# A decode block on one core: w_down in three transfers, a semaphore for each store, q in three chunks, nine matmuls fewer

## The chip, the cores and the metric

The kernel runs on one core of a Trainium2 chip. Its five engines are called by the profile's names: PE (TensorE, matmuls; PEld is its weight loads), DVE (VectorE), ACT (ScalarE), POOL (GpSimd) and SP (SyncE, which here only issues transfers). Sixteen DMA engines carry the transfers. The metric is the device time of one execution in microseconds (us); smaller is better.

## The reference

Two tokens (batch 2, one position each, width 640) pass through one block with modulation from a condition vector `c`. What is computed, shortened:

```python
mod = (silu(c) @ w_mod).reshape(2, 6, 1, -1)
sa, ca, ga, sb, cb, gb = (mod[:, i] for i in range(6))
h = layernorm(x) * (1 + ca) + sa
q = (h @ wq)                              # 32 heads of 192
p = softmax(q k^T * 192 ** -0.5)          # over the last 1024 cached keys
x = x + ga * ((p v) @ wo)
h = layernorm(x) * (1 + cb) + sb
x = x + gb * ((gelu(h @ w_gate) * (h @ w_up)) @ w_down)
```

All inputs are bfloat16. wq is 640 x 6144, wo 6144 x 640, w_gate and w_up 640 x 1536, w_down 1536 x 640, w_mod 640 x 3840. K and V have 32 heads per batch row, and 1024 rows of 192 of each head are used. That is 77 MB of reads for two tokens.

## The kernel before, in words

The scheduler in the kernel (`_Sched`) is a recorder: each operation is put into the list of its engine in the order in which the program calls it, with the operations that it depends on. At the end the lists are written out (`S.emit`), and each engine runs its list strictly in order, with a wait on a semaphore ahead of an operation where one is needed. All compute engines count on one semaphore each; each transfer, or group of transfers, has its own. One recorded operation can hold many matmuls, and those who wait for it wait for its last.

All large transfers are issued by SP from one list (every issue has line 378): w_mod, c, wq, four of K, four of V (6144 KB each), wo in two parts with eight small ones (`wx`) between, w_gate, w_up, w_down. A ring of slots in `store` is used again and again, so a later transfer waits until PE has read the slot's earlier contents.

The stages in order of time:

- Modulation and first LayerNorm (L510, L478 to L497), while w_mod and wq come in.
- **q** (L533): `hT` is the normalised input, transposed, in five parts of 128. PE's array is used as four column groups of 32, so group j makes the j-th quarter (1536 columns) of q. Each quarter is made in four chunks of `QC` = 384 columns, one in each of the PSUM banks 4 to 7: 5 x 4 x 4 = 80 matmuls. ACT and DVE copy the four chunks to `qC` in turn (L541, L543), a selection by 16 matmuls (L552) spreads q over the partitions, and ACT writes it to `qbc`. The third K transfer is issued after the q matmuls, since it overwrites wq.
- A loop of 57 matmuls that nobody reads (L691, L693) keeps PE busy until K arrives.
- **Scores**: for each half tile DVE multiplies K by `qbc` (L571), PE sums groups of columns with an identity matrix (L590), DVE finishes the sum (L604). Between them PE runs groups of four matmuls without a reader (L583).
- **Softmax and PV** (L610 to L637, L649), then the normalisation of the attention output (L662, L666) and its selection into rows: `p_sel(0)` and `p_sel(1)` (L674), eight matmuls each. Between the two stand `warm(3, 1)`, after the second `warm(6, 1)`: three and six matmuls of 384 columns into bank 1, which nobody reads (L563). The chunks are copied (L541, L543), transposed by DVE (L738, L744), and multiplied by wo (L782, in two groups with the sixteen `wx` matmuls of L790 between).
- **Second LayerNorm** (L799 to L497), then gate and up projections (L822), GELU (L829), the product (L836) and its transposes (L840).
- **Down projection** (L852): w_down has twelve rows of 1280 B on each partition, `WD_SPLIT = [6, 3, 2, 1]` says how many rows a transfer brings. Each transfer has its own semaphore, and the matmuls of a group of rows wait for it: eight matmuls for a row. `WD_WARM` gives the number of matmuls without a reader behind each group, all zero.
- **End**: DVE multiplies and adds (L861, L863), SP and ACT each store one half of the output (L378), both on the semaphore `sem_out`, and SP waits until it has 32 (L870).

Of the kernel before, what the change touches and what calls it, by code (L numbers as in the profile page):

```python
# [193 lines left out]
def bass_adaLN_cond__sliding_block_cached__geglu_ffn__decode_kernel(  # L194
# [21 lines left out]
    SQ = 32  # L216
# [17 lines left out]
    RN = HM * Dh  # L234
    QC = 2 * Dh
    NQC = RN // QC
    SCALE = float(Dh) ** -0.5
    EPS = 1e-5
    GC = 512 // JH
# [12 lines left out]
    assert sum(WO_SPLIT) == NB and sum(OT_SPLIT) == NB  # L252
    WU_SPLIT = [5]
    assert sum(WU_SPLIT) == KT
    WD_SPLIT = [6, 3, 2, 1]
    AT_SPLIT = [6, 6]
    assert sum(AT_SPLIT) == FT
    assert sum(WD_SPLIT) == FT
    NG = 2
# [5 lines left out]

    WO_WARM = [4, 9]
    WU_WARM = [5]
    WD_WARM = [0, 0, 0, 0]
    K_WARM = 14

    es = ExitStack()
    with es:
        S = _Sched(nc, es)
# [5 lines left out]
        wq_v = r1.rearrange("p (k n) -> p k n", k=KT)  # L279
# [12 lines left out]
        Qsel = aux_f(0, 2 * HM * P).rearrange("p (b m n) -> p b m n", b=2, m=HM)  # L292
        qC = aux_f(2 * HM * P, RN)
# [28 lines left out]
        sc = sb("sc", [P, DN], BF16)  # L322
# [9 lines left out]
        hT = sb("hT", [P, KT, SQ], BF16)  # L332
# [17 lines left out]
        ps = es.enter_context(nc.psum_tensor("ps", [P, 8, 512], F32))  # L350

        BK_T = 2
        BK_O = 3
        BK_C = 4
        BK_W = 4
        BK_H = 4
# [5 lines left out]
        def bank(k):  # L362
            return ("bank", k)
# [8 lines left out]
        sem_wu = [S.sem("d_wu%d" % i) for i in range(len(WU_SPLIT))]  # L372
        sem_wd = [S.sem("d_wd%d" % i) for i in range(len(WD_SPLIT))]
        sem_ring = [S.sem("d_ring%d" % i) for i in range(4)]
        sem_out = S.sem("d_out")

        def k_dma(dst, src):
            return lambda e: e.dma_start(dst, src)  # L378
# [5 lines left out]
        def dram_rows(v):  # L384
# [10 lines left out]
             reads=[("S", 0, 0, 0), ("S", 0, 0, 1), ("S", 0, 1, 0), ("S", 0, 1, 1)], writes=["ident_f"], name="ident_f")  # L395
        S.op("pool", lambda e: e.tensor_copy(out=ident_b[:, :], in_=ident_f[:, :]),
             reads=["ident_f"], writes=["ident_b"], name="ident_b")
# [4 lines left out]
             reads=["ident_f"], writes=["G32"], name="G32")  # L402
        S.op("dve", lambda e: e.tensor_reduce(out=M32[:, :], in_=ident_f[:, :].rearrange("p (h t) -> p h t", t=QP), axis=AX.X, op=ALU.add),
             reads=["ident_f"], writes=["M32"], name="M32")
# [3 lines left out]
             reads=["G32"], writes=["Bsel"], name="Bsel")  # L408
# [3 lines left out]
             reads=["M32"], writes=["DS"], name="DS")  # L412
# [4 lines left out]
             reads=["ident_f"], writes=["Osel"], name="Osel")  # L417
        for b in range(2):
            S.op("dve", (lambda b: lambda e: e.tensor_copy(
                out=SEL[:, b, :, BS * b:P:SQ], in_=G32[:, :].rearrange("p (j m) -> p m j", m=HM)))(b),  # L420
                reads=["G32"], writes=["SEL"], name="SEL%d" % b)
        for b in range(2):
            for m in range(HM):
# [3 lines left out]
                    reads=["ident_f"], writes=["Qsel"], name="Qsel%d%d" % (b, m))  # L427
# [7 lines left out]
        keep = {}  # L435
# [91 lines left out]
        for i, (ka, kb) in enumerate(wq_of):  # L527
            def f(e, ka=ka, kb=kb):
                last = None
                for k in range(ka, kb):  # L530
                    for c in range(NQC):
                        for j in range(NJ):
                            last = e.matmul(ps[SQ * j:SQ * j + SQ, BK_H + c, 0:QC], lhsT=hT[:, k, :],  # L533
                                            rhs=wq_v[:, k, RN * j + QC * c:RN * j + QC * (c + 1)],
                                            start=(k == 0), stop=(k == KT - 1), tile_position=(0, SQ * j), skip_group_check=True)
                return last
            keep["q"] = S.op("pe", f, reads=["hT", ("wq", i)], writes=[bank(BK_H + c) for c in range(NQC)], name="q%d" % i)

        def move(eng, dst, src, reads, writes, name):
            if eng == "act":  # L540
                S.op("act", lambda e: e.activation(out=dst, in_=src, func=ACTF.Copy), reads=reads, writes=writes, name=name)  # L541
            else:
                S.op("dve", lambda e: e.tensor_copy(out=dst, in_=src), reads=reads, writes=writes, name=name)  # L543

        for c in range(NQC):
            move(("act", "dve")[c % 2], qC[:, QC * c:QC * (c + 1)], ps[:, BK_H + c, 0:QC], [bank(BK_H + c)], [("qC", c)], "qC%d" % c)

        def f(e):
            last = None
# [2 lines left out]
                    last = e.matmul(ps[:, BK_O, b * Dh:(b + 1) * Dh], lhsT=Qsel[:, b, m, :], rhs=qC[:, m * Dh:(m + 1) * Dh],  # L552
                                    start=(m == 0), stop=(m == HM - 1), skip_group_check=True)
            return last
        S.op("pe", f, reads=[("qC", c) for c in range(NQC)] + ["Qsel"], writes=[bank(BK_O)], name="qsel")
        move("act", qbc[:, :, :].rearrange("p b d -> p (b d)"), ps[:, BK_O, 0:2 * Dh], [bank(BK_O)], ["qbc"], "qbc")
        load_kv(3, deps=keep["wq_dma"] + [keep["q"]])

        def warm(n, bk):
            def f(e):  # L560
                last = None
                for _ in range(n):
                    last = e.matmul(ps[:, bk, 0:2 * Dh], lhsT=ident_b[:, :], rhs=qbc[:, :, :].rearrange("p b d -> p (b d)"),  # L563
                                    start=True, stop=True)
                return last
            if n:
                S.op("pe", f, reads=["ident_b", "qbc"], writes=[bank(bk)], name="warm")
# [40 lines left out]
        def softmax(b):  # L608
# [8 lines left out]
            S.op("dve", lambda e: e.tensor_scalar(out=gx[:, :, :], in0=gm[:, :].unsqueeze(2).broadcast_to([1, H, QP]),  # L617
                                                  scalar1=-SCALE, scalar2=None, op0=ALU.mult),
                 reads=["gm"], writes=["gx"], name="gx%d" % b)
# [50 lines left out]
        def p_sel(b):  # L670
            def f(e):
# [4 lines left out]
                return last  # L676
            S.op("pe", f, reads=["SEL"] + [("On", b, g) for g in range(NJ)], writes=[bank(BK_H + c) for c in range(NQC)], name="sel%d" % b)

# [48 lines left out]
            if t == NTL - 1:  # L727
                p_sel(0)
        normalize(1)
        warm(3, 1)  # L730
        p_sel(1)
        warm(6, 1)
        assert keep["kv"] == len(items)
        for c in range(NQC):
            move(("act", "dve")[c % 2], oc[:, QC * c:QC * (c + 1)], ps[:, BK_H + c, 0:QC], [bank(BK_H + c)], [("oc", c)], "oc%d" % c)
        t0 = 0
        for i, nt in enumerate(OT_SPLIT):
            S.op("dve", (lambda t0, nt: lambda e: e.transpose(oT[:, t0:t0 + nt, :], oc.rearrange("p (q k) -> p k q", k=NT)[:, t0:t0 + nt, :]))(t0, nt),  # L738
                 reads=[("oc", c) for c in range(NQC)], writes=[("oT", t) for t in range(t0, t0 + nt)], name="oT%d" % i)
            t0 += nt  # L740
        oc_x = oc.rearrange("p (h b a k) -> p k h a b", h=2, a=XQ, k=NT)
        for h in range(2):
            for j in range(NJ):
# [3 lines left out]
                    reads=[("oc", c) for c in range(NQC)], writes=[("oX", h, j)], name="oX%d%d" % (h, j))  # L747
# [3 lines left out]
        for i, (ta, tb) in enumerate(wo_of):  # L751
            S.dma("sp", k_dma(wo_v[:, ta:tb, :].rearrange("p t n -> p (t n)"), wo_src[:, ta:tb, :].rearrange("p t n -> p (t n)")),
                  sem_wo[i], writes=[("wo", i)], deps=[keep["pv", 0, t] for t in (NTL - 2, NTL - 1)], name="ld_wo%d" % i)
            if i == 0:
                wx_src = A_wo.rearrange("(j h b a t) n -> t j h a b n", j=NJ, h=2, a=XQ, t=NT)
                for h in range(2):
                    for j in range(NJ):
                        S.dma("sp", k_dma(wx[SQ * h:SQ * h + XQ * XQ, D * j:D * (j + 1)], wx_src[NB, j, h]), sem_wx,
                              writes=[("wx", h, j)], deps=[keep["pv", 0, NTL - 1], wx0], name="ld_wx%d%d" % (h, j))
# [3 lines left out]
              writes=["wg"], deps=r3_dead, name="ld_wg")  # L763
# [13 lines left out]
        for i, (ta, tb) in enumerate(wo_of):  # L777
# [16 lines left out]
            if i == 1:  # L794
# [5 lines left out]
             reads=[bank(BK_M), ("modC", 0)], writes=[("lnt", 0)], name="ga_attn")  # L800
        S.op("dve", lambda e: e.tensor_tensor(out=X2[:, 0, :], in0=lnt[:, 0, :], in1=X2[:, 0, :], op=ALU.add),
             reads=[("lnt", 0)], writes=[("X2", 0)], name="x1")
        layer_norm("ln2", 1, 3)

        def f(e):
            last = None
            for i, v in enumerate((X2[:, 0, :], modC[:, 5, :])):
# [6 lines left out]
             reads=[bank(BK_X), ("modC", 0)], writes=["xg"], name="xg")  # L814
        warm(8, 1)

        def ffn_gu(bk, wv, key, name, ka, kb):
            def f(e):
# [11 lines left out]
             reads=[bank(BK_G[0])], writes=["gl"], name="gelu")  # L830
        k0 = 0
        for ci, nk in enumerate(WU_SPLIT):
# [4 lines left out]
             reads=[bank(BK_G[1]), "gl"], writes=["aC"], name="geglu")  # L837
        f0 = 0
        for i, nf in enumerate(AT_SPLIT):
            S.op("dve", (lambda f0, nf: lambda e: e.transpose(aT[:, f0:f0 + nf, :].rearrange("p f (i b) -> p f b i", b=2 * NH),  # L840
                                                              aC.rearrange("p (q f) -> p f q", f=FT)[:, f0:f0 + nf, :]))(f0, nf),
                 reads=["aC"], writes=[("aT", r) for r in range(f0, f0 + nf)], name="aT%d" % i)
            f0 += nf
        f0 = 0
        for ci, nf in enumerate(WD_SPLIT):
            def f(e, f0=f0, nf=nf):
# [15 lines left out]
             reads=[bank(BK_C), "xg"], writes=[("lnt", 1)], name="gb_y")  # L862
        S.op("dve", lambda e: e.tensor_tensor(out=sc[0:OR, 0:DO], in0=lnt[0:OR, 1, 0:DO], in1=modC[0:OR, 0, 0:DO], op=ALU.add),  # L863
             reads=[("lnt", 1), "xg"], writes=["sc"], name="outC")
        for g, eng in enumerate(("sp", "act")):
            S.dma(eng, k_dma(out[:, 0, :].rearrange("b (v g n) -> (b v) g n", v=NH, g=NG)[:, g, :], sc[SQ * g:SQ * g + 2 * NH, 0:DO]),
                  sem_out, reads=["sc"], name="st_out%d" % g)

        S.emit("sp", nc.sync)
        nc.sync.wait_ge(sem_out, 16 * NG)  # L870
        S.emit("pool", nc.gpsimd)
        S.emit("act", nc.scalar)
        S.emit("dve", nc.vector, hinted_end=True)
# [29 lines left out]
```

## Time and profile before

| | |
|---|---|
| median of 3 runs | 186.21 us (186.15 to 186.33) |
| the profiled execution | 186.49 us |
| its span in the profile | 185.1 us |
| read from memory | 76.88 MB, 415 GB/s over the span |
| busy: PE, DVE, ACT, POOL | 122.9, 111.0, 14.1, 7.1 us |
| mean granted clock of PE | 0.945 |

A profile is of one execution. "Busy" is the time in which an engine worked. "Granted clock" is the share of PE's full clock that it got. The chain of waits is followed back from the last instruction: each step to what released it. A row of the waits says who waited for whom, for how long in all, how often, and the longest. A row of stretches gives for each engine the busy time in that stretch with the number of instructions that touch it. "DMA share" is the mean busy share of the sixteen DMA engines; it can be a little over 1, since a packet is put into the stretch in which it begins. A transfer lands when all of its DMA engines have added to its semaphore.

### The profile page before, as it was taken

The page shows a single profiled execution, that of the slowest core. Times are in us where ns is not written, and L with a number is a line of the kernel's source. Part 1 is how long each engine was busy: PE and PEld are TensorE (multiplying, and loading weights), DVE is VectorE, ACT ScalarE, POOL GpSimd, SP SyncE. Part 2 cuts the span into 40 slices and gives each one's busy share as a digit, 9 for nine tenths or more (in the row PEclk, how much of TensorE's full clock was granted, in tenths as well). Part 3 has the DMA queues.
Part 4 walks back from the last instruction along what each step waited for, and adds up shares of the span by engine and source line. Part 5 has one row for each costly group of instructions (what it writes and reads, how often), then busy time and mean ns, then how long its engine had stood idle before and what let it go on. Part 6 is the DMA issues. An engine that isn't in the chain of part 4 may idle for free.

```text
span 185.1 us, 2753 instructions
## 1 busy us (share of the span) xinstructions
PE 122.9 (66%) x1123; PEld 67.2 (36%) x1123; DVE 111.0 (60%) x124; ACT 14.1 (8%) x25; POOL 7.1 (4%) x14
## 2 busy tenths in 40 slices
PE   0004500878989989889898895399739039749864
PEld 0001200445534444434444342256426027447423
DVE  5941600020499999999999993749195500593623
ACT  2002300023000000000000000101100000510310
POOL 8600000000000000000000000000000000000000
PEclk9999999999999999999999999579978858979999
DMA  7999999898989999998989898989999899999992
GB/s 257 407 425 452 465 465 430 372 492 351 499 372 489 404 446 446 404 489 361 499 351 499 351 510 351 499 354 489 425 425 471 372 430 425 404 431 427 427 388 86
DMA packets 2814, 76.98 MB, mean 416 GB/s; under 512 B 376, under 2 KB 632, under 8 KB 1016
## 3 DMA queue, kind: packets, MB, share of 16 engines
q1 hardware_dynamic: 2780, 76.88, 97.0%
q8 instruction: 6, 0.10, 0.2%
q10 hardware_dynamic: 28, 0.00, 0.0%
HBM read 76.88 MB, written 0.00 MB: 415 GB/s over the span
## 4 chain that ended last, share of the span: by engine, by line
DMA 38%; DVE 35%; PE 15%; SPq 8%; issue 1%; ACT 1%; POOL 1%; DVEq 0%; POOLq 0%
DVE store L571 27%; DMA store<-in_A_k_cache_dram 25%; DMA store<-in_B_w_down_dram 13%; PE ps L649 11%; SPq L378 8%; DVE Sg L604 5%; PE ps L590 3%; DVE Em L637 2%; PE ps L629 0%; DVE On L666 0%; ACT On L662 0%; PE ps L583 0%; PE ps L852 0%; PE ps L621 0%; ACT E_sb L626 0%
## 5 line engine op out<-in xcount | busy, mean ns | idle before, releaser
L571 DVE TENSOR_TENSOR store<-store,qbc 128x6144 bf16<-128x6144 bf16 x16 | 53.5, 3346 | 9.0 <-DMA store<-in_A_k_cache_dram 9.0
L590 PE MATMUL ps<-store,ident_b 128*128 x192 | 44.2, 380 | 6.2 <-DVE store L571 6.2
L649 PE MATMUL ps<-store,Em 128*64 128x384 bf16 x256 | 26.4, 372 | 13.7 <-DMA store<-in_A_v_cache_dram 7.1
L590 PEld LDWEIGHTS ps<-store,ident_b 128*128 128x128 bf16 x192 | 18.7, 97 | 29.6 <-issue 11.5
L649 PEld LDWEIGHTS ps<-store,Em 128*64 128x64 bf16 x256 | 16.4, 126 | 22.5 <-issue 7.4
L637 DVE TENSOR_TENSOR Em<-E_sb,M32b 128x2048 bf16<-128x2048 bf16 x8 | 18.1, 2283 | 2.5 <-PE ps L649 2.5
L510 PE MATMUL ps<-store,scT 128*32 128x480 bf16 x40 | 4.4, 602 | 15.4 <-DVE scT L467 15.4
L583 PE MATMUL ps<-qbc,ident_b 128*128 128x384 bf16 x64 | 13.0, 326 | 0.8 <-DVE store L571 0.8
L533 PE MATMUL ps<-store,hT 128*32 128x384 bf16 x80 | 5.5, 459 | 11.2 <-DMA store<-in_A_wq_dram 11.2
L604 DVE TENSOR_REDUCE Sg<-ps 128x32 f32<-128x512 f32 x16 | 10.9, 682 | 2.7 <-PE ps L590 2.7
L543 DVE CAST aux<-ps 128x384 bf16<-128x384 f32 x4 | 2.0, 553 | 16.9 <-PE ps L533 15.9
L666 DVE TENSOR_SCALAR On<-ps,rden 32x192 bf16<-32x192 f32 x4 | 1.7, 418 | 15.8 <-ACT On L662 15.8
L691 PE MATMUL ps<-qbc,ident_b 128*128 128x384 bf16 x56 | 9.3, 326 | 0.8 <-ACT qbc L541 0.8
L583 PEld LDWEIGHTS ps<-qbc,ident_b 128*128 128x128 bf16 x64 | 6.2, 98 | 6.7 <-issue 1.1
L533 PEld LDWEIGHTS ps<-store,hT 128*32 128x32 bf16 x80 | 3.1, 130 | 14.2 <-issue 12.1
L563 PE MATMUL ps<-qbc,ident_b 128*128 128x384 bf16 x40 | 7.7, 327 | 0.0
L626 ACT ACTIVATE E_sb<-Sg,nb 128x256 bf16<-128x256 f32 x2 | 1.0, 508 | 83.4 <-DVE nb L625 83.4
L510 PEld LDWEIGHTS ps<-store,scT 128*32 128x32 bf16 x40 | 1.2, 133 | 16.9 <-DVE scT L467 15.4
L782 PE MATMUL ps<-store,aux 128*32 128x160 bf16 x188 | 5.0, 281 | 3.1 <-DVE aux L738 3.1
L691 PEld LDWEIGHTS ps<-qbc,ident_b 128*128 128x128 bf16 x56 | 5.4, 98 | 4.5 <-issue 1.0
L782 PEld LDWEIGHTS ps<-store,aux 128*32 128x32 bf16 x188 | 4.6, 120 | 3.6 <-issue 3.5
L405 DVE CAST M32b<-M 128x32 bf16<-128x32 f32 x1 | 5.4, 5408 | 0.0
(85 smaller groups left out, 72.7 us busy)
## 6 DMA issues: line engine op xcount, KB each, us to landing
store<-in_A_k_cache_dram SPq DMA_DIRECT2D x4, 6144.0 KB, 40.1
store<-in_A_v_cache_dram SPq DMA_DIRECT2D x4, 6144.0 KB, 23.9
store<-in_A_wq_dram SPq DMA_DIRECT2D x1, 7680.0 KB, 31.1
store<-in_A_wo_dram SPq DMA_DIRECT2D x1, 5120.0 KB, 30.1
store<-in_w_mod_dram SPq DMA_DIRECT2D x1, 4800.0 KB, 14.2
store<-in_A_wo_dram SPq DMA_DIRECT2D x1, 2400.0 KB, 30.2
store<-in_B_w_gate_dram SPq DMA_DIRECT2D x1, 1920.0 KB, 29.5
store<-in_B_w_up_dram SPq DMA_DIRECT2D x1, 1920.0 KB, 33.8
```

The costliest lines, as they stand in the source:

```text
L378: return lambda e: e.dma_start(dst, src)
L510: last = e.matmul(ps[SQ * j:SQ * j + SQ, bk, 0:3 * DN].rearrange("p (i n) -> p i n", i=3), lhsT=scT[:, k, :], rhs=wm_v[:, k, 3 * part * D: ...
L533: last = e.matmul(ps[SQ * j:SQ * j + SQ, BK_H + c, 0:QC], lhsT=hT[:, k, :], rhs=wq_v[:, k, RN * j + QC * c:RN * j + QC * (c + 1)], start=( ...
L563: last = e.matmul(ps[:, bk, 0:2 * Dh], lhsT=ident_b[:, :], rhs=qbc[:, :, :].rearrange("p b d -> p (b d)"), start=True, stop=True)
L571: S.op("dve", lambda e: e.tensor_tensor(out=tile_v(ks)[:, hf * JH:(hf + 1) * JH, :], in0=tile_v(ks)[:, hf * JH:(hf + 1) * JH, :], in1=qbc[ ...
L583: last = e.matmul(ps[:, BK_W, 0:2 * Dh], lhsT=ident_b[:, :], rhs=qbc[:, :, :].rearrange("p b d -> p (b d)"), start=True, stop=True)
L590: last = e.matmul(o_ap, lhsT=ident_b[:, :], rhs=tile[:, hf * JH:(hf + 1) * JH, ci * GC:(ci + 1) * GC], start=(ci == 0), stop=(ci == NCH - 1))
L604: S.op("dve", lambda e: e.tensor_reduce(out=S_sb[:, b, a:a + JH], in_=ps[:, hf, 0:JH * GC].rearrange("p (j c) -> p j c", j=JH), axis=AX.X, ...
L637: S.op("dve", lambda e: e.tensor_tensor(out=Em[:, t % 2, :, :], in0=E_sb[:, b, J * t:J * (t + 1)].unsqueeze(2).broadcast_to([P, J, H]), in ...
L649: last = e.matmul(ps[r:r + 2 * H, BK_O, 0:ON], lhsT=Em[:, t % 2, 2 * jp:2 * jp + 2, :].rearrange("p j c -> p (j c)"), rhs=tile_v(vs)[:, 2 ...
L691: e.matmul(ps[:, BK_W, 0:2 * Dh], lhsT=ident_b[:, :], rhs=qbc[:, :, :].rearrange("p b d -> p (b d)"), start=True, stop=True)
L782: last = e.matmul(ps[SQ * j:SQ * j + SQ, BK_M, 0:DN], lhsT=oT[:, t, :], rhs=wo_v[:, t, DN * j:DN * j + DN], start=(t == 0), stop=(t == NB ...
```

## The change

Four edits. w_down's twelve rows come in three transfers of 6, 4 and 2 rows, where there were four of 6, 3, 2 and 1; the matmuls are grouped in the same way. Each of the two stores at the end has its own semaphore, and SP waits for 16 on each in turn. The q projection works in chunks of 512 columns, three of them, in the banks 4 to 6, with three copies (ACT, DVE, ACT) for four; the chunks of the attention output, which had the same size constant, stay at 384. The matmuls without a reader between and after the two selections, three and six, are gone.

```diff
+    QW = 512
+    NQW = RN // QW
+    assert NQW * QW == RN
...
-    WD_SPLIT = [6, 3, 2, 1]
+    WD_SPLIT = [6, 4, 2]
...
-    WD_WARM = [0, 0, 0, 0]
+    WD_WARM = [0, 0, 0]
...
-        sem_out = S.sem("d_out")
+        sem_out = [S.sem("d_out%d" % g) for g in range(NG)]
...
-                    for c in range(NQC):
+                    for c in range(NQW):
                         for j in range(NJ):
-                            last = e.matmul(ps[SQ * j:SQ * j + SQ, BK_H + c, 0:QC], lhsT=hT[:, k, :],
-                                            rhs=wq_v[:, k, RN * j + QC * c:RN * j + QC * (c + 1)],
+                            last = e.matmul(ps[SQ * j:SQ * j + SQ, BK_H + c, 0:QW], lhsT=hT[:, k, :],
+                                            rhs=wq_v[:, k, RN * j + QW * c:RN * j + QW * (c + 1)],
...
-        for c in range(NQC):
-            move(("act", "dve")[c % 2], qC[:, QC * c:QC * (c + 1)], ps[:, BK_H + c, 0:QC], [bank(BK_H + c)], [("qC", c)], "qC%d" % c)
+        for c in range(NQW):
+            move(("act", "dve")[c % 2], qC[:, QW * c:QW * (c + 1)], ps[:, BK_H + c, 0:QW], [bank(BK_H + c)], [("qC", c)], "qC%d" % c)
...
         normalize(1)
-        warm(3, 1)
         p_sel(1)
-        warm(6, 1)
...
-                  sem_out, reads=["sc"], name="st_out%d" % g)
+                  sem_out[g], reads=["sc"], name="st_out%d" % g)
...
-        nc.sync.wait_ge(sem_out, 16 * NG)
+        for g in range(NG):
+            nc.sync.wait_ge(sem_out[g], 16)
```

## The prediction

> **What bounds the kernel now.** I read the slices first, then the chain, then the waits, then stretches of the tail. All times are microseconds from the span's start unless marked ns.
>
> ```profile
> PEclk9999999999999999999999999579978858979999
> DMA  7999999898989999998989898989999899999992
> ```
>
> The DMA row is 8 or 9 from the second slice to the last but one: the 16 DMA engines move 76.88 MB without a pause until about 180. The granted clock dips after slice 29. The chain of waits ends so:
>
> ```profile
> 158.93 23.38 DMA store<-in_B_w_down_dram
> 182.31 0.04 issue
> 182.35 0.73 PE ps L852 x24
> 183.09 0.02 issue
> 183.11 0.24 DVE lnt L861
> 183.36 0.02 issue
> 183.38 0.23 DVE sc L863
> ```
>
> So the end is set by the landing of w_down, then by the matmuls of L852 that need its last rows, two small DVE operations and the stores (issued at 183.64, over at 185.1). What happens earlier counts only if it delays a transfer or arrives late at this tail. The table of waits tells how much room there is:
>
> ```profile
> DVE store L571 <- DMA store<-in_A_k_cache_dram: 9.0, 1, 9.0
> ...
> PE ps L822 <- DMA store<-in_B_w_up_dram: 1.0, 1, 1.0
> ```
>
> After q is done DVE still waits 9.0 for the first K transfer; and everything from the attention output to the second LayerNorm arrives 1.0 ahead of w_up. Busy time by stretch (columns: length, PE, PEld, DVE, ACT, POOL with counts, granted clock, DMA share, GB/s):
>
> ```profile
> 157.05:160.47 3.42, 2.82 (x29) 1.93 (x26) 0.94 (x3) 0.92 (x3) 0.00 (x0) 1.00 0.89 383
> 160.47:163.88 3.41, 0.84 (x6) 0.29 (x3) 3.31 (x4) 2.05 (x3) 0.00 (x0) 1.00 0.96 399
> 163.88:167.29 3.41, 2.85 (x88) 2.89 (x92) 3.19 (x10) 0.00 (x0) 0.00 (x0) 0.50 1.01 431
> ...
> 177.50:180.25 2.75, 1.91 (x25) 0.85 (x25) 1.04 (x2) 0.00 (x0) 0.00 (x0) 1.00 0.99 396
> 180.25:182.30 2.05, 1.46 (x72) 1.31 (x72) 1.34 (x2) 0.00 (x0) 0.00 (x0) 1.00 0.58 227
> 182.30:183.10 0.80, 0.71 (x24) 0.47 (x24) 0.00 (x0) 0.00 (x0) 0.00 (x0) 1.00 0.00 0
> ```
>
> From 180.25 the DMA share is only 0.58: some engines are finished and some are late. The trace's landing records (one increment per DMA engine) say it exactly: for the last w_down transfer six engines report between 180.70 and 181.41, ten between 182.20 and 182.71. The late ten set the end.
>
> **w_down in 6, 4, 2 rows instead of 6, 3, 2, 1.** The bytes are the same. Each row of a transfer is one packet per partition, so each DMA engine carries 8 packets per transfer and one small packet for the semaphore. The packet records give 55 ns for 1280 B, 102 ns for 2560 B and 149 ns for 3840 B: 47 ns for each 1280 B and 8 ns that are left for the packet itself; the 4 B packet takes 9 ns. One transfer fewer saves 8 x 8 + 9 = 73 ns on every engine, the late ones too. Bounds: the last increments of the four transfers come at 180.35, 181.51, 182.31 and 182.71, that is 0.39, 0.40 and 0.40 per row, which shows no cost per transfer at all (gain 0); the most would be the whole last step, 0.40, but PE is then the limit: its 72 earlier weight loads end at 182.14, 24 more at 18 ns end at 182.57 instead of 182.93, a gain of at most 0.36. I take 0.07, from the packets themselves.
>
> Against it: behind the last landing stand two rows, 16 matmuls, where there was one row, 8 matmuls. The tail in detail (L852 alone; PE, PEld, clock, DMA):
>
> ```profile
> 182.34:182.66 0.32, 0.30 (x16) 0.31 (x16) 1.00 0.00 0
> 182.66:182.74 0.08, 0.08 (x10) 0.00 (x1) 1.00 0.00 0
> 182.74:182.93 0.19, 0.19 (x12) 0.17 (x8) 1.00 0.00 0
> ```
>
> Sixteen weight loads, a gap until the last row is there (182.71), then eight. The instructions start in pairs every 36 ns, so eight more cost 8 x 18 ns = 0.14. Bounds: 0 if the rows land early enough that PE never waits; 0.24 at the 30 ns each of the chain's row (0.73 / 24). Taken: +0.14. The rows before them do not bind: the 4-row transfer lands at about 181.51 + 0.40 = 181.9; PE has done the first 48 matmuls by 180.83 + 0.86 = 181.7, waits 0.2, does 32 in 0.58 and is free at 182.5, ahead of the last landing at 182.64. What is late next, should w_down come earlier, is that PE chain. Net of the part: +0.07.
>
> **Two store semaphores.** SP waits twice instead of once, and nothing is queued behind. The last increment of the second store comes at 185.06 either way. SP's gaps between instructions are 0.04 to 0.05, so 0 to 0.05; a shared semaphore at 32 also waits for both, so no gain. Taken: +0.02. The number of semaphores and waits on SP is otherwise the same (w_down has one fewer).
>
> **q in three chunks.** 60 matmuls of 512 columns for 80 of 384; per column group 5 x 3 x 512 = 5 x 4 x 384 = 7680 columns. The 80 take 5.54; bounds 4.2 (by count) and 7.4 (by length of one, if the count did not matter); I take 5.5. The copies: ACT moved 2 x 384 in 0.87, now 2 x 512, 1.16 by the column; DVE moved 2 x 384 in 1.02, now one of 512. The later of the two goes from 1.02 to 1.16. So qbc (42.02) moves by -1.3 to +2.0. DVE's wait of 9.0 covers it; without that cover it would cost its +0.14. PE's loop of dummy matmuls ends at 51.7, 0.75 ahead of the first real reduction at 52.45, which waits for DVE; if qbc were 2.0 later the first warm round would be 1.2 late, and the reductions recover inside DVE's chain, whose end does not set the transfers. The third K transfer on SP's queue waits for the q matmuls (38.8): in front of it are two K transfers that land at 48.8 and 63.3, so the DMA engines do not notice. Taken: 0.
>
> **Nine matmuls fewer.** Three stood between the two selection groups (0.65 of PE) where PE then still waits 0.60 for the normalised rows from ACT and DVE; the second group starts at 159.50 all the same. Six (1.14) stood after it; PE then waits 3.1 for the transposes, now 4.1. No instruction reads their bank in between. Removed work: nothing on the path. What it may cost is the clock: in 160.47 to 163.88 PE is busy for 0.84 of 3.41, now it would be 0, and in the next stretch the granted clock is 0.50 already. Taken: 0, since that half clock is in the time before.
>
> The Trainium skill, in TensorE: Matmul & The Clock Gate, "What you observe", has the half clock after an idle window of about 3.4 us, and advises against idle gaps over about 3 us; this speaks against taking the six out. The trace agrees on the half clock, but has it with a gap of 3.1 and the six in place, so by that rule too the sum stays at 0 unless the stretch at half clock grows; that is the second rival below.
>
> **Sum.** -0.07 + 0.14 + 0.02 = +0.09 to the profiled execution of 186.49 (span 185.1, 1.4 around it), so 186.58. The median of the runs before is 186.21, 0.28 below the profiled execution; on the median's basis the forecast is 186.21 + 0.09 = 186.3. A difference under 0.2% (0.37) is about what a measurement of this kernel can tell from no change.
>
> **Rivals.**
>
> 1. *Slower: an instruction refill falls on a late DMA engine.* The instruction queue has 6 packets of 16 KB in the span, at 39.5, 123.1, 141.7, 163.2, 170.7 and 178.8. One costs its engine over 1: after the one at 39.5, 15 engines have the first K transfer by 47.70 and one at 48.76. PE's program has 29 matmuls with their loads, 58 instructions, fewer, so refills that follow PE's progress come later in the work: the last would move from the up projection into L852, at about 181. If it falls on one of the six engines that are finished it is free, as now; on one of the ten that still move w_down it adds 1.06 to 1.5 to the last landing. That gives 187.3 to 187.8. For it: the shift is certain, the place is not. [...] Chance 0.12.
> The Trainium skill, in Runtime: NRT & Kernel Launch, has refills in 16 KiB blocks of 256 instructions; the trace's six packets agree in size.
>
> 2. *Slower: the half clock lasts longer.* At half clock the 88 matmuls counted in 163.88 to 167.29 take 32 ns each; the 60 of the second projection group take 1.22, 20 ns each. If the half clock lasts to the end of that group, some 116 matmuls pay 12 ns and four long ones 0.12 each: 1.9. From 1.03 on, w_up no longer covers it: up to +0.9, 186.7 to 187.2. Against it: the next stretch of PE work is as dense as before. Chance 0.08.
>
> 3. *Faster: a transfer costs more than its packets.* Then the last landing comes up to 0.40 earlier and PE is the limit: 185.9 to 186.1; beyond 0.2% only if the bound of 0.36 is beaten by something in the tail that I do not see. Chance 0.12, of which 0.07 beyond 0.2%.
>
> That the change does not do what it says is excluded by the instruction lists of the two kernels: they differ in these places and nowhere else.
>
> **How the numbers follow.** Forecast 0.68, rivals 0.12, 0.08 and 0.12. Faster by over 0.2%: 0.07. Slower: 0.12 + 0.08 = 0.20. Within: 0.73. The forecast with its bounds (gain 0 to 0.36, cost 0 to 0.29) runs from 185.85 to 186.5; reaching into the second rival up to 186.9 leaves out no more than 2 in 10: 185.9 to 186.9.
>
> **What would show it.** Right: in the chain after, w_down lands near 182.6 and PE L852 x16 follows in about 0.5; the wait of L822 for w_up stays near 1.0; DVE's first wait for K stays near 9. Wrong: w_down's landing moves by over 0.3 either way, the wait of L822 is gone (then look at the granted clock from 164 to 171), or a packet of the instruction queue stands in the window from 180.3 to 182.3.

## The result and the profile after

The changed kernel takes 187.53 us (median; 186.27 to 189.06, 20 runs), the kernel before on the same chip 186.22 (185.97 to 187.83, 20 runs). The ratio is 1.0064, with a 95% interval of 1.0047 to 1.0080: slower by 1.2 us. The forecast was 186.3, the range 185.9 to 186.9. The profiled execution took 188.11, with a span of 186.8 (before: 186.49 and 185.1). For four kernels below (`e1`, `e4`, `e10`, `e15`) the comparison leaves the slower runs out as disturbed, though their traces show the cause that is studied; so the median of all their runs is given too.

The slices of the changed kernel first, the granted clock and the DMA share:

```profile
PEclk9999999999999999999999998599969657957999
DMA  7999999899998989999898999989899899999970
```

The DMA row is full until the same place; the clock has more dips. The end of the chain of waits (in order of time: start, length, engine, tile, line):

```profile
165.77 4.46 PE ps L783 x128
170.23 0.76 PE ps L566 x4
170.98 0.38 PE ps L791 x15
171.37 0.92 issue
172.29 0.23 PE ps L791
172.51 1.18 PE ps L783 x60
...
178.30 1.00 PE ps L823 x20
...
181.85 1.02 DVE aT L841
...
182.92 1.91 PE ps L853 x96
184.82 0.02 issue
184.85 0.24 DVE lnt L862
185.09 0.02 issue
185.11 0.23 DVE sc L864
```

Before, the last link ahead of the tail was the landing of w_down. Here no transfer stands in these rows: all 96 matmuls of w_down run after `aT`, one behind the other, 1.91. The landing records say that w_down's last increment came at 182.40, even earlier than before (182.71); w_up's came earlier too, at 177.77 for 178.01. So the compute chain from the wo projection to the end has become late, and in it stands a step of 0.92 named "issue": PE waits for nothing that the profile shows. The waits name the place, and the two that the prediction spoke of:

```profile
DVE store L574 <- DMA store<-in_A_k_cache_dram: 9.6, 1, 9.6
...
PE ps L791 <- issue: 0.9, 1, 0.9
```

The wait of the up projection for w_up, 1.0 before, has gone. PE's instructions in order of time (start, busy time, the idle time before in brackets), before and after:

```profile
164.44 3.75 PE L782 MATMUL ps<-store,aux 128*32 128x160 bf16 x128 [3.13 <-DVE aux L738]
168.12 0.82 PE L563 MATMUL ps<-qbc,ident_b 128*128 128x384 bf16 x4
168.87 0.46 PE L790 MATMUL ps<-wx,oX 64*32 64x160 bf16 x16
169.26 1.22 PE L782 MATMUL ps<-store,aux 128*32 128x160 bf16 x60
```

```profile
165.77 4.46 PE L783 MATMUL ps<-store,aux 128*32 128x160 bf16 x128 [4.10 <-DVE aux L739]
170.16 0.82 PE L566 MATMUL ps<-qbc,ident_b 128*128 128x384 bf16 x4
170.91 0.45 PE L791 MATMUL ps<-wx,oX 64*32 64x160 bf16 x15
172.29 0.23 PE L791 MATMUL ps<-wx,oX 64*32 64x160 bf16 x1 [0.92 <-issue]
```

The sixteen `wx` matmuls are one recorded operation. PE does fifteen, stands still for 0.92 and does the last. Nothing in the program lies between the fifteenth and the sixteenth, so it is likely the instructions that are missing. The instruction queue fits that: in a window of 0.6 us the trace has one packet of it, before from 163.0 (it starts at 163.24) and after from 169.5 (at 169.74):

```profile
q8 instruction: 1, 0.02, 10.1%
```

```profile
q8 instruction: 1, 0.02, 11.1%
```

The packet comes 6.5 us later; it lasts 1.07 us, and PE goes on 1.48 after its end. **Numbers.** To see which instructions it brings, count PE's own list in program order: a matmul is two (its weight load and itself), a float32 matmul four, a separate wait or a branch one. The sixteenth `wx` matmul of the changed kernel is 1222 and 1223. Every stop below lies at 1223 or 1479, 256 apart, and the packets are 16 KB. So borders lie at 967, 1223 and 1479, and the packet at 163.24 or 169.74 brings what begins at 1223. The Trainium skill (Runtime: NRT & Kernel Launch, "Instruction fetch mechanics") has the same 256 instructions in a block of 16 KiB. The change takes 58 instructions away, 40 with q and 18 with the nine matmuls. That puts the wait for the transposes of the attention output (the one ahead of the wo matmuls) at number 926, where it was 984; between them lies the border 967.

**Theory.** PE asks for the block at 1223 when its reading has come far enough past 967. Before, that happens ahead of the long wait for the transposes, and the idle time of 3.13 covers the packet, which ends 0.23 before the wo matmuls start; after, PE stands in that wait at 926, asks only when it is released, and is out of instructions before the block is there. **Rivals:** the clock (the stretch at half clock from 163.29 to 170.12 makes the wo matmuls 4.46 long where they took 3.75), and the tail of w_down.

### The profile page after: what moved, and what is told of

It is laid out like the page before. It is cut to its first block, busy times and chain, and to the rows that moved or that the text cites. A ratio compares the mean times of both kernels' runs of the same rounds, so it can differ in the third digit from the quotient of the medians.

```text
span 186.8 us, 2693 instructions
## 1 busy us (share of the span) xinstructions
PE 122.8 (66%) x1094; PEld 66.7 (36%) x1094; DVE 110.6 (59%) x123; ACT 14.3 (8%) x25; POOL 7.2 (4%) x14
## 4 chain that ended last, share of the span: by engine, by line
DVE 39%; DMA 38%; PE 19%; issue 2%; ACT 1%; POOL 1%; SPq 0%; DVEq 0%; POOLq 0%
DVE store L574 26%; DMA store<-in_A_k_cache_dram 25%; DMA store<-in_A_v_cache_dram 13%; PE ps L652 8%; DVE Sg L607 5%; PE ps L783 3%; PE ps L593 3%; DVE aux L739 1%; DVE Em L640 1%; PE ps L823 1%; PE ps L853 1%; PE ps L566 1%; DVE aux L546 1%; DVE aT L841 1%; DVE On L669 0%
## 5 line engine op out<-in xcount | busy, mean ns | idle before, releaser
L652 PE MATMUL ps<-store,Em 128*64 128x384 bf16 x256 | 27.5, 382 | 14.1 <-DMA store<-in_A_v_cache_dram 7.4
L652 PEld LDWEIGHTS ps<-store,Em 128*64 128x64 bf16 x256 | 17.1, 129 | 23.1 <-issue 7.8
L586 PE MATMUL ps<-qbc,ident_b 128*128 128x384 bf16 x64 | 13.0, 326 | 1.1 <-DVE store L574 1.1
L536 PE MATMUL ps<-store,hT 128*32 128x512 bf16 x60 | 5.3, 532 | 11.1 <-DMA store<-in_A_wq_dram 11.1
L546 DVE CAST aux<-ps 128x384 bf16<-128x384 f32 (+1 forms) x3 | 1.7, 599 | 16.5 <-PE ps L536 15.5
L694 PE MATMUL ps<-qbc,ident_b 128*128 128x384 bf16 x56 | 9.3, 326 | 0.8 <-ACT qbc L544 0.8
L783 PE MATMUL ps<-store,aux 128*32 128x160 bf16 x188 | 5.7, 305 | 4.1 <-DVE aux L739 4.1
L536 PEld LDWEIGHTS ps<-store,hT 128*32 128x32 bf16 x60 | 2.2, 128 | 14.5 <-issue 14.1
L783 PEld LDWEIGHTS ps<-store,aux 128*32 128x32 bf16 x188 | 5.2, 131 | 5.6 <-issue 5.6
L566 PE MATMUL ps<-qbc,ident_b 128*128 128x384 bf16 x31 | 5.9, 328 | 0.0
L739 DVE STREAM_TRANSPOSE aux<-aux 128x512 bf16<-128x512 bf16 (+1 forms) x3 | 4.0, 1397 | 0.1
```

Source lines behind the costliest of these rows:

```text
L536: last = e.matmul(ps[SQ * j:SQ * j + SQ, BK_H + c, 0:QW], lhsT=hT[:, k, :], rhs=wq_v[:, k, RN * j + QW * c:RN * j + QW * (c + 1)], start=( ...
L586: last = e.matmul(ps[:, BK_W, 0:2 * Dh], lhsT=ident_b[:, :], rhs=qbc[:, :, :].rearrange("p b d -> p (b d)"), start=True, stop=True)
L652: last = e.matmul(ps[r:r + 2 * H, BK_O, 0:ON], lhsT=Em[:, t % 2, 2 * jp:2 * jp + 2, :].rearrange("p j c -> p (j c)"), rhs=tile_v(vs)[:, 2 ...
L694: e.matmul(ps[:, BK_W, 0:2 * Dh], lhsT=ident_b[:, :], rhs=qbc[:, :, :].rearrange("p b d -> p (b d)"), start=True, stop=True)
L783: last = e.matmul(ps[SQ * j:SQ * j + SQ, BK_M, 0:DN], lhsT=oT[:, t, :], rhs=wo_v[:, t, DN * j:DN * j + DN], start=(t == 0), stop=(t == NB ...
```

## The experiments

No edit changes what a kernel computes. "Tiny" matmuls have 2 columns and 32 weight columns, no reader, and stand ahead of q, where PE has time. A group of n of them moves every later number by 2n - 1: two for each, less one separate wait that PE no longer needs (its trace has 17 instead of 18). They are written so:

```python
def f(e):
    last = None
    for _ in range(29):
        last = e.matmul(ps[0:SQ, 1, 0:2], lhsT=ident_b[:, 0:SQ], rhs=ident_b[:, 0:2], start=True, stop=True)
    return last
S.op("pe", f, reads=["ident_b"], writes=[bank(1)], name="pad")
```

**The parts alone.** `e5`: before, with w_down and the stores as changed. `e4`: before, with q in three chunks. `e3`: before, without the nine matmuls. The lines that show it, shortened:

```diff
# e3
-        warm(3, 1)
         p_sel(1)
-        warm(6, 1)
# e4
-                    for c in range(NQC):
+                    for c in range(NQW):
...
# e5
-    WD_SPLIT = [6, 3, 2, 1]
+    WD_SPLIT = [6, 4, 2]
...
-                  sem_out, reads=["sc"], name="st_out%d" % g)
+                  sem_out[g], reads=["sc"], name="st_out%d" % g)
...
```

> The kernel before, with w_down in three transfers and a semaphore for each store (only these two edits; PE's list keeps its length). Theories refill and clock: 1.000 to 1.001 of before (the forecast's +0.09). Theory tail: 1.0064.

> The kernel before, with q in three chunks of 512 (only that edit). Theory refill: 40 instructions fewer put the boundary at about the tenth matmul of the output projection; PE uses the block up 118 matmuls later, at about 169, while the refill needs some 6 from request to use: a wait of 1 to 2 there, 1.003 to 1.008. Theories clock and tail: 1.000.

> The kernel before, without the nine matmuls around the second selection (only that edit). Theory refill: the boundary comes 9 matmuls later in the work, still ahead of the output projection, so no wait: 1.000 to 1.002. Theory clock: 1.003 to 1.008, with the half clock in the output projection longer than before. Theory tail: 1.000.

Measured: `e5` 186.34, ratio 1.0003 (0.9983 to 1.0024), no stop. `e4` 187.82, 1.0075 (1.0046 to 1.0104), with a stop of 1.35 after 6 `wx` matmuls. `e3` 189.19, 1.0138 (1.0103 to 1.0172), with the longest stop so far, 2.53, after the 128 matmuls of the first wo group:

```profile
164.93 3.97 PE L780 MATMUL ps<-store,aux 128*32 128x160 bf16 x128 [4.10 <-DVE aux L736]
171.43 1.27 PE L563 MATMUL ps<-qbc,ident_b 128*128 128x384 bf16 x4 [2.53 <-issue]
172.63 0.72 PE L788 MATMUL ps<-wx,oX 64*32 64x160 bf16 x16
```

So the nine matmuls alone make the kernel slower than all four edits together, q alone about as much as all four, and w_down with the stores costs nothing that can be measured. In `e3` the first of the four dummies is number 1223, in `e4` the seventh `wx` matmul is 1222 and 1223. The expectation that `e3` would run without a stop was wrong; so was the position that it worked with.

**The numbers alone.** `e1`: the changed kernel with 29 tiny matmuls. `e2`: before with 99. `e6`: changed with 45. `e7`: before without the nine, with 25. `e8`: before with 16, a control.

> The changed kernel, with 29 tiny matmuls without a reader (2 columns, 32 weight columns) early, while PE waits for wq: PE's program up to the output projection is again as long as in the kernel before, all four edits stay. Theory refill (the program is 58 PE instructions shorter, so PE enters a 256-instruction block in the middle of the output projection instead of in the idle time before it, and waits 0.9 for the next block): the refill packet is back near 163, the 0.9 of idle before the last wx matmul is gone, time 1.000 to 1.003 of before. Theory clock (without the nine matmuls PE runs the output projection at half clock for longer): unchanged, 1.005 to 1.008. Theory tail (two rows behind the last landing): unchanged, 1.0064.

> The kernel before, with 99 tiny matmuls without a reader early: 198 instructions more is 58 fewer modulo 256, so the block boundaries lie as in the changed kernel, and nothing else is changed. Theory refill: a wait of 0.9 to 1.8 inside or right after the wx matmuls, refill packet near 169, time 1.003 to 1.007 of before. Theories clock and tail: 1.000.

> The changed kernel with 45 tiny matmuls early, 16 more than in the run with 29. In the runs so far PE stopped each time ahead of instruction 1223 of its list (counting a matmul as two), and the refill began 3.8 to 4.1 after the output projection started, so the request must have come only when PE got past the wait for the transposes. With 45 the block that precedes it is entered 32 instructions earlier, in the last PV group, well ahead of that wait. Theory refill: refill packet before 163, no idle of PE in the output projection or wx, 0.999 to 1.003 of before. Theory clock (the missing nine matmuls cost by themselves): 1.003 to 1.008. If the run with 29 was slow because of the tiny matmuls themselves: 1.008 or more.

> The kernel before without the nine matmuls, with 25 tiny ones early: from the output projection on, every instruction has the number that it has in the run with 45 and in the control with 16. Theory refill: the 1.0138 of the run without the nine falls to 1.000 to 1.003. Theory clock: it stays above 1.005, with the half clock in the output projection.

> Control: the kernel before, all nine matmuls kept, with 16 tiny ones early; the same block boundaries as in the two runs beside it. Theories refill and clock: 1.000, refill packet before 163. If tiny matmuls early cost by themselves: slower by what the others show.

Measured: `e6` 186.45, ratio 1.0003 (0.9987 to 1.0018); `e7` 186.30, 0.9992 (0.9972 to 1.0013); `e8` 186.23, 0.9991 (0.9975 to 1.0007); no stop in any. `e2` 186.97, 1.0038 (1.0012 to 1.0064), a stop of 1.51 at 1479, the next border: a kernel that loses none of its work, and gains only tiny matmuls, gets the same kind of stop. Its runs spread from 186.25 to 188.62 (the profiled one took 188.47), so some executions hardly pay for it. `e1` went against the expectation: 189.70, 1.0087 (1.0044 to 1.0129), a stop of 2.37.

`e6` is the best comparison, since its profiled execution had the same stretches of half clock as that of the changed kernel (146.26 to 156.50 and 163.33 to 170.16; after: 146.22 to 156.46 and 163.29 to 170.12). PE in `e6`, and the end of its chain:

```profile
165.90 4.42 PE L790 MATMUL ps<-store,aux 128*32 128x160 bf16 x128 [4.10 <-DVE aux L746]
170.26 0.82 PE L573 MATMUL ps<-qbc,ident_b 128*128 128x384 bf16 x4
171.01 0.46 PE L798 MATMUL ps<-wx,oX 64*32 64x160 bf16 x16
171.40 1.22 PE L790 MATMUL ps<-store,aux 128*32 128x160 bf16 x60
```

```profile
181.87 1.91 PE ps L860 x96
...
184.07 0.23 DVE sc L871
```

The wo matmuls are as slow (4.42 for 4.46) and start 0.13 later; without the stop the second wo group starts at 171.40 instead of 172.44, and the last operation at 184.07 instead of 185.11. Both differences are 1.04. With the same four edits and the numbers moved, the kernel is back at the time before; the rival of the clock falls as the cause of the 1.2 us, and that of the tail with it.

**Where the border must lie.** `e9` and `e11` move the wait for the transposes to 982 and 985 (`warm(5, 1)` behind the second selection, in `e11` with two tiny matmuls), `e10` is the changed kernel with 30 tiny.

> The kernel before with five matmuls instead of six after the second selection: one matmul fewer, nothing else. It brings the wait for the transposes from 17 to 15 instructions behind number 967, where the block ahead of the stop at 1223 begins. The run with 29 tiny matmuls had 16 and was slow, the kernel before has 17 and is not. Theory distance (the request for the next block goes out only some 17 instructions into a block, and a wait before that holds it back): slow, 1.008 to 1.015, refill packet near 168.5. Theory entry (the request goes out when the block is entered; the run with 29 was slow for another reason, such as the missing nine): 1.000, refill packet near 163. Theory clock: 1.000 to 1.001.

> The kernel before with five matmuls instead of six, and two tiny ones early, which bring the wait to 18 instructions behind number 967. Theory distance: fast again, 1.000. If five matmuls are too few in themselves: as slow as the run without the two.

> The changed kernel with 30 tiny matmuls early, one more than in the slow run with 29: the wait for the transposes is 18 instructions behind number 967. Theory distance: fast, 0.999 to 1.003, refill packet near 163, although the nine matmuls are missing. Theory entry with a cost of the missing nine: slow as with 29, 1.008 or more.

Measured: `e9` 186.21, 0.9997 (0.9984 to 1.0011); `e11` 186.36, 1.0003 (0.9988 to 1.0019), both without a stop. `e10`: 189.89, the median of 6 runs from 186.28 to 190.19 (it has no ratio), a stop of 2.21. `e10` and `e11` have the wait at the same number, 985, with opposite outcomes: a fixed distance doesn't decide. Six further kernels took that up: the nine as tiny ones (`e13`), the changed kernel with 36 tiny (`e14`), all nine matmuls between the selections (`e15`) or behind (`e16`), `e16` with 4 tiny (`e17`), before with 6 tiny (`e18`).

```diff
# e13
-        warm(3, 1)
+        tiny(3)
         p_sel(1)
-        warm(6, 1)
+        tiny(6)
# e15
-        warm(3, 1)
+        warm(9, 1)
         p_sel(1)
-        warm(6, 1)
# e16
-        warm(3, 1)
         p_sel(1)
-        warm(6, 1)
+        warm(9, 1)
```

> The kernel before with the nine matmuls of 384 columns replaced by nine of 2 columns (32 weight columns), at the same places. All of PE's instruction numbers stay as in the kernel before (the wait for the transposes is at 984), only the time that PE works between the two selections and after them falls from 1.8 us to about 0.3. Count theory (the request for the next block of instructions goes out once some 20 or more instructions have gone by after the wait for the second token's rows): 34 instructions go by, so the refill packet stands near 163, PE does not stop in the wo matmuls, ratio 1.000. Time theory (PE has to work for over about 1 us behind that wait): the packet stands near 168.5, PE stops 1 to 2.5 ahead of number 1223, ratio 1.006 to 1.014.

> The changed kernel with 36 tiny matmuls ahead of q instead of 29, 30 or 45. The wait for the transposes is at 997, the wait for the second token's rows at 980, and the block border 967 lies in the first selection (964 to 979), which PE does some 1.5 us before the second one. Border theory (the request needs the border to be crossed in a run of instructions that ends in some other wait than that for the transposes): packet before 163.5, no stop, ratio 1.000. Count theory (only the 16 instructions after the last wait but one count): packet near 168.5, a stop of over 1, ratio 1.006 to 1.014.

> The kernel before with all nine matmuls without a reader between the two selections and none after them. Numbers: border 967 is the wait for the second token's rows, the second selection is 968 to 983, the wait for the transposes is at 984 as in the kernel before. Distance theory: nothing changes, packet near 163, ratio 1.000. Count and time theories: only 16 instructions, 0.8 us of work, come after the wait for the second token's rows, so the packet stands near 168.5, PE stops for 1 to 2.5, ratio 1.006 to 1.014.

> The kernel before with all nine matmuls without a reader behind the second selection and none between. Numbers: the wait for the second token's rows at 949, the second selection 950 to 965, the nine 966 to 983, the wait for the transposes at 984. Count, time and distance theories: 34 instructions and 2.5 us of work behind the wait for the second token's rows, packet near 163, no stop, ratio 1.000. If it is late all the same (packet near 168.5, ratio 1.006 to 1.014), all three fall, and what counts is the place of the border itself.

> The kernel before with all nine matmuls behind the second selection (the order that was late with the wait for the transposes at 984) and four tiny matmuls ahead of q, so that every number is 7 higher: the wait for the second token's rows at 956, the second selection 957 to 972, the nine 973 to 990, the wait for the transposes at 991. Zone theory (with that wait at 981 or earlier the request is late, from some 990 on early, between them it goes either way): packet near 163 to 164, no stop, ratio 1.000. Theory of the place (the border must lie in the second selection, 956 to 971 as in the kernel before): early too. Theory of the order (nine matmuls behind the second selection are late by themselves): packet near 169, a stop of over 1 ahead of number 1223, ratio over 1.006.

> The kernel before with six tiny matmuls ahead of q and its selections and matmuls without a reader as they were, so that every number is 11 higher: the wait for the second token's rows at 966, the second selection 967 to 982, the six behind it, the wait for the transposes at 995. Zone theory: 995 is beyond the zone, packet near 163, no stop, ratio 1.000. Theory of the place: the wait for the second token's rows stands right at the border, as in the two padded versions of the changed kernel that were late (966 and 968), so packet near 168.5, a stop of over 1 ahead of number 1223, ratio over 1.006.

All kernels by the number of the wait for the transposes. "Packet" is the start of the one that brings 1223 (in `e2` that of 1479, whose wait is put down relative to its own border); "goes on" is the time from the first wo matmul until PE is past the border.

| kernel | wait, past the border by | packet | stop | goes on | ratio (95% interval) |
|---|---|---|---|---|---|
| `e2` | 1181, -42 | 170.27 | 1.51 | 6.65 | 1.0038 (1.0012 to 1.0064) |
| changed | 926, -41 | 169.74 | 0.92 | 6.52 | 1.0064 (1.0047 to 1.0080) |
| `e4` | 944, -23 | 168.60 | 1.35 | 6.39 | 1.0075 (1.0046 to 1.0104) |
| `e3` | 966, -1 | 169.00 | 2.53 | 6.50 | 1.0138 (1.0103 to 1.0172) |
| `e9` | 982, 15 | 163.54 | none | | 0.9997 (0.9984 to 1.0011) |
| `e1` | 983, 16 | 169.08 | 2.37 | 6.44 | 1.0087 (1.0044 to 1.0129) |
| before | 984, 17 | 163.24 | none | | 1 |
| `e5` | 984, 17 | 164.07 | none | | 1.0003 (0.9983 to 1.0024) |
| `e13` | 984, 17 | 163.43 | none | | 0.9988 (0.9967 to 1.0009) |
| `e15` | 984, 17 | 168.38 | 2.29 | 6.04 | 1.0100 (1.0017 to 1.0183) |
| `e16` | 984, 17 | 170.08 | 3.33 | 6.66 | 1.0217 (1.0172 to 1.0262) |
| `e11` | 985, 18 | 163.19 | none | | 1.0003 (0.9988 to 1.0019) |
| `e10` | 985, 18 | 168.44 | 2.21 | 6.07 | (189.89) |
| `e17` | 991, 24 | 164.13 | none | | 1.0016 (0.9999 to 1.0033) |
| `e18` | 995, 28 | 162.82 | none | | 1.0017 (0.9992 to 1.0042) |
| `e14` | 997, 30 | 160.49 | none | | 1.0009 (0.9990 to 1.0028) |
| `e12` | 1000, 33 | 161.82 | none | | 1.0003 (0.9986 to 1.0020) |
| `e6`, `e7`, `e8` | 1015, 48 | 160.44, 158.88, 158.95 | none | | 1.0003, 0.9992, 0.9991 |

(`e15`'s median of all runs is 189.38, from 186.81 to 189.95; `e16`'s 190.65.) What follows: with the wait ahead of the border, the packet comes late in all four kernels; with the wait 24 or more past it, it comes early in all seven; at 15 to 18 past it goes either way. The count theory falls with `e16` (34 instructions, late), the time theory with `e13` (its dummies take 0.53 us in all where they took 1.79, early), the theories of the place and of the order with `e18` and `e17` (both early, as the zone theory expected). `e14` came out as the border theory expected, but the kernel before doesn't fit that theory: its border lies in the second selection, in the run of instructions that ends in the wait for the transposes, and its packet is early. Among the kernels at 15 to 18 the number doesn't decide, and what does stays open. Single runs of `e1` (186.56), `e10` (186.28) and `e15` (186.81), and one of the changed kernel (186.27), are as fast as those without a stop; that would fit an outcome that varies from run to run, but these runs have no trace. `e15` and `e16`, with the same numbers and nearly the same instructions as the kernel before, show how close to the edge that kernel stands. PE in `e16`:

```profile
165.93 3.33 PE L781 MATMUL ps<-store,aux 128*32 128x160 bf16 x119 [2.64 <-DVE aux L737]
172.59 0.58 PE L781 MATMUL ps<-store,aux 128*32 128x160 bf16 x9 [3.33 <-issue]
```

and in `e18`:

```profile
164.28 3.81 PE L790 MATMUL ps<-store,aux 128*32 128x160 bf16 x128 [3.13 <-DVE aux L746]
168.02 0.82 PE L571 MATMUL ps<-qbc,ident_b 128*128 128x384 bf16 x4
```

**A version that could be faster.** `e12` is `e5` with loops of dummy matmuls, which cost few numbers (33 matmuls in PV, 17 behind the second selection), to keep the full clock.

> A candidate: the kernel before with w_down in three transfers and the two store semaphores, and two loops of matmuls without a reader that keep PE busy while it waits: 33 ahead of the third PV group of the second token, 17 in place of the six after the second selection. The wait for the transposes is 33 instructions behind number 967. Expected: no refill stop, no half clock from 144 to 170, wait for w_up about 3, the time as that of the undisturbed runs of the kernel before in all of its runs: 0.998 to 1.000. If the loops hold PE up or their branches cost: over 1.002.

Measured 186.47, 1.0003 (0.9986 to 1.0020). The granted clock is 1.00 from 141.68 to 168.99 and the first wo group takes 2.40 instead of 3.75, but then the second waits for its weights:

```profile
168.64 1.91 PE L794 MATMUL ps<-store,aux 128*32 128x160 bf16 x60 [1.93 <-DMA store<-in_A_wo_dram]
```

PE's gain is a wait for a transfer; the end is still set by the DMA engines, with the landing of w_down at 182.43. No version beat both kernels.

## Why the prediction was wrong, point by point

- **What bounds the kernel** was read rightly for the kernel before: arrival 1.0 ahead of w_up, then the landing of w_down. The margin of 1.0 was the figure to guard, and the change used it up.
- **w_down, -0.07 and +0.14**: from the last increment of w_up to the last of w_down it is 4.63 in the changed kernel and 4.67 in `e5`, against 4.70 before. But the spread between the kernels is as large: the seven with three transfers have 4.63 to 4.70 (mean 4.66), the thirteen with four 4.64 to 4.71 (4.68). So a gain of 0.02 is what can be read, the -0.07 is not shown, and nothing is left of rival 3. The landing itself moved by 0.31, a sign of being wrong by the prediction, but 0.24 of it is w_up's, which landed earlier as well. The +0.14 for 16 matmuls behind the last landing could not be seen, since in both profiles `aT` came last; `e5`'s ratio bounds the whole part and the stores to -0.3 to +0.4 us.
- **Two store semaphores, +0.02**: within the same bound.
- **q in three chunks, "Taken: 0"**: the local working held. The 60 matmuls took 5.3 (5.5 forecast), DVE's wait for K was 9.6. But alone it costs 0.75% (`e4`), because 40 instructions fewer move the wait from 984 to 944.
- **Nine matmuls fewer, "Removed work: nothing on the path. Taken: 0"**: this is the step that failed, with that of q: the two terms put at 0 hold nearly the whole 1.2. The work of the nine is on the median indeed worth nothing: `e13` keeps nine matmuls with 0.53 of PE time for 1.79 and loses nothing. Their eighteen numbers are worth 1.4% (`e3`), and with 25 tiny matmuls elsewhere the cost is gone (`e7`). With the numbers moved, all four edits together measure 1.0003 (`e6`) and 1.0009 (`e14`), which leaves room for the +0.09 of the sum. An instruction that does nothing useful was priced by its time alone.
- **Rival 1, the instruction refill**: the prediction counted the 58 instructions and the six packets and said that the shift was certain. It looked for the cost in the DMA engine that carries the packet. That did not happen: the packet at 180.27 left the last landing where it was. The cost lies in PE, which waits for the packet. That its 187.3 to 187.8 contains the 187.53 is chance. The question that was not asked: when is each packet needed, and by which number?
- **Rival 2, half clock**: its sign, no wait for w_up and a longer half clock, was in the profile after, and in a part of the executions this rival is real. `e5` and `e6` were profiled with the half clock of PV at nearly the same place (146.04 to 156.28 and 146.26 to 156.50). In `e5`, with the nine, PE is busy for 2.33 of the stretch 159.69 to 163.11, and the next half clock lasts 3.41. In `e6`, without them, it is busy for 0.83 of 159.91 to 163.33, and the half clock lasts 6.83; the first wo group takes 4.42 for 3.77, and the span is 186.0 for 185.2. Of the 34 runs of `e6`, `e7` and `e14` (no nine, no stop) nine have a mean clock of 0.926 or 0.927 and a median of 187.03, inside the 186.7 to 187.2 of the rival; the other 25 have 186.36. None of the 125 runs of the kernel before that were taken beside the experiments is under 0.935. But over all their runs the three kernels are at 1.0003, 0.9992 and 1.0009, so the 1.2 of the changed kernel is not the clock's.
- **The rule of the Trainium skill that was weighed** (no idle gaps over about 3 us; it stands in TensorE: Matmul & The Clock Gate, "Why this matters for your kernels", not in the section that the prediction named): `e7` has no dummies behind the second selection, a gap of 4.10, and half clock for 3.41 as before; `e6` has the same gap and half clock for 6.83. So the rule bites in some executions, as under rival 2, and not on the median.
- **What the Trainium skill says of refills** (Runtime: NRT & Kernel Launch, "Instruction fetch mechanics"): the cost of crossing a block is one queue operation, mostly hidden. Most packets here are hidden; that at 1223 (in `e2` at 1479) is not in eight of the twenty kernels, with stops of 0.92 to 3.33. The measurement decides.

## What to carry to other kernels

An instruction without effect still holds a place: before adding or taking away instructions on PE, count where each block of 256 begins, and let PE's long waits stand well past a border (24 numbers or more were safe here; at 15 to 18 it went either way, and ahead of the border none was). Where a profile shows an engine idle inside one run of instructions with "issue" as the cause, look for the packet of the instruction queue just before it ends; a few tiny instructions early in the program, where the engine has time, move the border, and tell by one run whether that is the cause. A part that is slower alone than with the others can be a sign of position, not of work.

## What the runs showed of the hardware

- From the first wo matmul to the late packet it was 3.6 to 4.2 us in all eight kernels that were late, and PE went on after 6.0 to 6.7. In seven that were early with the border behind the wait for the second token's rows, the one ahead of the second selection (before, `e5`, `e9`, `e11`, `e13`, `e17`, `e18`) the packet came 3.3 to 4.0 after the start of the second selection. So a packet comes some 4 us after the release of the wait that held the reading back, here with all sixteen DMA engines at work.
- The stop is what is left of those 6 to 6.7 us: PE reaches 1223 early in `e3`, right after the 128 wo matmuls (2.53), and late in the changed kernel, 19 matmuls further (0.92). That fits with the nine and q together costing less than the nine alone.
- A stop can take the clock down: in `e3` the granted clock is 0.50 from 171.67 to 175.08, and the second wo group takes 2.06 instead of 1.22.
- The clock changes on a grid of 3.41 us, whose place against the program differs between executions: in `e7` 0.50 from 146.97 to 153.80, in `e6` from 146.26 to 156.50. The Trainium skill (TensorE: Matmul & The Clock Gate, "What's actually happening") calls this window free-running and gives 3413 ns; the traces agree. Over the 20 traces, from 115 us on, a full clock was halved after each of the 63 stretches of that grid in which PE was busy for 43% or less, and kept after each of the 195 with 49% or more. In the kernels without the nine the place is worth some 0.7 of an execution (the 187.03 and 186.36 above), which is why one profile alone could not tell the 0.92 of the stop from the rest of its 1.7.
